# Weight-gradient partials of w2: from a DRAM round trip to sums held open in PSUM, with layer 1's 1−tanh on VectorE

## The chip, the cores and the metric

The kernel runs on one core of one Trainium2 chip. The metric is the device time of one launch in microseconds; lower is better. Engine names as in the profile: PE is the tensor engine (PEld its weight loads), DVE the vector engine, ACT the scalar engine, POOL GpSimd, SP the sync engine. POOL, SP and ACT also issue DMAs, each from its own queue of instructions.

## The reference

The model has two layers, each a gated long convolution (A) and an MLP (B), both with a residual and a LayerNorm ahead of them. S = 2048, D = 448, F = 1792, all inputs bf16. The kernel computes the output and the gradients of all inputs but the constant `B_x`, for a given `grad_out`.

```python
def _A_ref(q, k, v, shift_k, ssm_k, ssm_D):
    k_shift = ...                      # 4-tap causal shift convolution of k
    kv = k_shift * v
    kv_f, kf_f = rfft(kv, 2S), rfft(ssm_k, 2S)
    y = irfft(kv_f * kf_f)[:S] + kv * ssm_D
    return q * y
def _B_ref(x, w1, w2):
    return silu(x @ w1) @ w2
x = A_q
x = x + _A_ref(_layernorm(x), A_k, A_v, A_shift_k, A_ssm_k, A_ssm_D)
x = x + _B_ref(_layernorm(x), B_w1, B_w2)
x = x + _A_ref(_layernorm(x), A_k, A_v, A_shift_k, A_ssm_k, A_ssm_D)
x = x + _B_ref(_layernorm(x), B_w1, B_w2)
out, vjp = jax.vjp(f, ...); return (out, *vjp(grad_out))
```

The gradient of `w2`, a matrix of 1792 x 448, is the sum over both layers of (silu activations, transposed) times (the gradient at the layer's output). In each layer that is a contraction over the 2048 positions. The gradient of `w1` has the same form.

## The kernel before

The convolution's result y is the same in both layers (it does not depend on x), so it is computed once, in a prefix (0 to about 97 us of the trace). `Main` then runs layer 0 forward (about 97 to 212), layer 1 forward with layer 1 backward interleaved (to about 420), and layer 0 backward (to about 554). `_ssm_suffix` takes the gradient gYb, summed over both layers, through the FFT convolution backward and does the rest of the weight gradients.

**Main.** The 2048 positions are four chunks of 512. For one chunk, `h` multiplies by w1 (ps_h, L556), takes tanh (L560) and silu (L561) on ACT, and forms the derivative dT on DVE (L564, L569, L570). Between them stands 1−tanh: in layer 1 it is on ACT (L566), in layer 0 on DVE (L568). `out` multiplies by w2 (ps_o, L588). `ga` (ps_g, L618) multiplies the output gradient by w2T; ACT copies that out of PSUM (L624), DVE multiplies it by dT (L625). `gn` (ps_n, L659) multiplies by w1T and goes through the backward of two LayerNorms on DVE, per 128 positions: ACT reads ps_n into lb_u (L661), and DVE runs `ln_bwd` (L639 to L643) and L668 to L671. w2T and w1T lie in the pool "mwt", which closes when Main ends.

**Weight gradients.** One sum for 128 rows of w2 (index ft, 0 to 13) is ps_d: 16 matmuls of 128x448, one for each 128 positions, with the activations (dstat, 512 KB, loaded by SP from DRAM, for half of layer 0's by a transposing DMA) as the stationary side and the output gradient as the moving side. For layer 1 (activations A_d1) the moving side is grad_out; for layer 0 (activations A0_d) it is mov2, the gradient at layer 0's output, cast at L697.

- `_wgrad_w2_first` makes the mov2 x A0_d part for ft 0 to 9 at the end of Main and for ft 10 to 13 after FFT stage 1 in the suffix. ACT copies each ps_d to dpo in fp32 (L804), and POOL stores it in W2P_d (L805, 224 KB).
- `_wgrad_rest` makes the grad_out x A_d1 part (L795) from the spectrum stage on. It loads the partial again (dpart, L816, on SP), adds it on DVE (L821) and stores the bf16 result. After that come the w1 sums: both layers' parts in one PSUM sum of 32 matmuls, then a cast (L826), transposes (L829), a scaled copy on ACT (L831) and a store.

**Suffix.** FFT stage 1 is `_fft_stage1` (ps_s, L209; it needs M1s, loaded on POOL, and gYb) with its copy to A1g; then transposes (ps_tr, L873); then, for seven pairs of chunks (cp), `spectrum` (L883), the products pa and pb with kk_c (L908, L909; kk_c is loaded on POOL by `kernel_part`, L893 and L894) and the inverse matmuls (ps_v, L229 and L230). Then gK (L949), gkv, sk (L980), gk (L998). POOL also loads ksf (L896, at cp 2) and mov3 (L898, at cp 4). The ps_d matmuls have no fixed places among this: a scheduler orders the instructions, and may put them between others. `issue_after` gives the earliest place.

PSUM places go by tags with two buffers each: "mm" (ps_h, ps_g, ps_s, ps_tr and most of the suffix), "tr" (ps_t, ps_d) and "po" (ps_o, ps_n, ps_sk, ps_dt).

The lines that decide a sum:

```python
def fin_w2(ft, ps, part):
    o = pool.tile([P, D], BF16, name="dout", tag="dout", bufs=4)
    nc.vector.tensor_tensor(out=o[:], in0=ps[:, :D], in1=part[:], op=ALU.add)
    nc.gpsimd.dma_start(out=k.outs[8][ft * P:(ft + 1) * P, :], in_=o[:])
```

Of the kernel before, what the change touches and what calls it, by code (L numbers as in the profile page):

```python
# [10 lines left out]
FP32 = mybir.dt.float32  # L11
# [6 lines left out]
P = 128  # L18
S = 2048
D = 448  # L20
# [100 lines left out]
def kernel(  # L121
# [41 lines left out]
    k.W2P_d = dram.tile([F, D], FP32, name="W2P_d")  # L163
# [20 lines left out]
    with tc.tile_pool(name="yk", bufs=1, side="right") as yk:  # L184
        k.Ysb = yk.tile([P, J, D], BF16, name="Ysb")
        _ssm_prefix(k)
        k.w1sb = k.wk.tile([DC, ND, F], BF16, name="w1sb", tag="WA")
        nc.sync.dma_start(out=k.w1sb[:], in_=k.B_w1.rearrange("(c p) f -> p c f", p=DC))
        k.w2sb = k.wk.tile([P, NF, D], BF16, name="w2sb", tag="WB")
        nc.sync.dma_start(out=k.w2sb[:], in_=k.B_w2.rearrange("(c p) d -> p c d", p=P))  # L190
        k.psum = ctx.enter_context(tc.tile_pool(name="psum", bufs=1, space=PSUM, reuse_waits="tile"))
        k.bal.reset()
        with ExitStack() as es:
            m = Main(k, es)
            m.run()
            with tc.issue_after(k.d0_load.ins):
                _wgrad_w2_first(k, m.td, range(10))
# [48 lines left out]
def _pm(ap2d):  # L246
    return ap2d.rearrange("(p j) d -> p j d", j=J)
# [30 lines left out]
def _ssm_prefix(k):  # L278
# [4 lines left out]
    with ExitStack() as es:  # L283
# [16 lines left out]
        ksb += [k.dp.tile([DC, S], BF16, name="K_sb", tag="dstat", bufs=2)[:] for i in range(2)]  # L300
# [116 lines left out]
        k.x0c0 = k.dp.tile([P, 4, D], BF16, name="x0c0", tag="dstat", bufs=2)  # L417
        nc.gpsimd.dma_start(out=k.x0c0[:], in_=_pm(k.A_q[0])[:, 0:4, :])
        k.na0 = k.dp.tile([P, 4, D], BF16, name="na0", tag="dstat", bufs=2)
# [41 lines left out]
class Main:  # L461

    def __init__(self, k, es):
        self.k, self.nc, self.tc = k, k.nc, k.tc
        nc, tc = k.nc, k.tc
        pool = lambda name, **kw: es.enter_context(tc.tile_pool(name=name, bufs=1, reuse_waits="tile", **kw))
        self.wt = pool("mwt")
        self.w2T = self.wt.tile([P, ND, F], BF16, name="w2T")
        self.w1T = self.wt.tile([P, NF, D], BF16, name="w1T")
        self.td = pool("mtd")  # L470
        self.ch = pool("mch")
        self.xp = pool("mx", side="right")
        self.X = self.xp.tile([P, NT, D], FP32, name="X")
        self.w1sb, self.w2sb, self.Y = k.w1sb, k.w2sb, k.Ysb
# [71 lines left out]
    def h(self, c, L, nT, half, hold):  # L546
# [4 lines left out]
        for ft0, n in ((0, 2), (2, 2), (4, 2), (6, 1)) if half == 0 else ((7, 1), (8, 2), (10, 2), (12, 2)):  # L551
# [13 lines left out]
            if L == 1:  # L565
                nc.scalar.activation(tm, tm, ACT.Copy, scale=-1.0, bias=1.0)  # L566
            else:
                nc.vector.tensor_scalar(out=tm, in0=tm, scalar1=-1.0, scalar2=1.0, op0=ALU.mult, op1=ALU.add)  # L568
# [203 lines left out]
def _wgrad(k, pool, bridge, groups, consume, pre=None, alt=False, fts=range(NF)):  # L772
    nc, psum = k.nc, k.psum
    movs = []
    for (stat, mov_src), tag in groups:
        if tag is None:
            movs.append(mov_src)
            continue
        mov = k.wk.tile([P, NT, D], BF16, name="dmov", tag=tag)
        nc.sync.dma_start(out=mov[:], in_=mov_src)  # L780
        movs.append(mov)
    job = -1
    for ft in fts:
        ps = psum.tile([P, 512], FP32, name="ps_d", tag="tr", bufs=2)
        aux = pre(ft) if pre else None
        for gi, ((stat, _), _) in enumerate(groups):
            job += 1
            if pool is None or (job % 2 == 0 if alt else job < bridge or job % 5 < 2):
                pl, bf, tg = k.dp, 2, "dstat"
            else:  # L790
                pl, bf, tg = (pool, 2, "S") if alt else (pool, 3, "dstat")
            st = pl.tile([P, NT, P], BF16, name="dstat", tag=tg, bufs=bf)
            _load_stat(k, st, stat, ft)
            for t in range(NT):
                nc.tensor.matmul(ps[:, :D], lhsT=st[:, t, :], rhs=movs[gi][:, t, :], start=(gi == 0 and t == 0), stop=(gi == len(groups) - 1 and t == NT - 1))  # L795
        consume(ft, ps, aux)


def _wgrad_w2_first(k, pool, fts):
    nc, dp = k.nc, k.dp  # L800

    def consume(ft, ps, aux):
        o = dp.tile([P, D], FP32, name="dpo", tag="dpart", bufs=3)
        nc.scalar.copy(o[:], ps[:, :D])  # L804
        nc.gpsimd.dma_start(out=k.W2P_d[ft * P:(ft + 1) * P, :], in_=o[:])  # L805

    _wgrad(k, pool, 0 if pool else NF, [((k.A0_d, k.mov2), None)], consume, alt=pool is not None, fts=fts)


def _wgrad_rest(k, pool, after, mov3):  # L810
    nc, dp, psum = k.nc, k.dp, k.psum
    out7v = k.outs[7].rearrange("(c p) f -> p c f", p=DC)

    def pre(ft):
        part = dp.tile([P, D], FP32, name="dpart", tag="dpart", bufs=3)
        nc.sync.dma_start(out=part[:], in_=k.W2P_d[ft * P:(ft + 1) * P, :])  # L816
        return part

    def fin_w2(ft, ps, part):
        o = pool.tile([P, D], BF16, name="dout", tag="dout", bufs=4)  # L820
        nc.vector.tensor_tensor(out=o[:], in0=ps[:, :D], in1=part[:], op=ALU.add)  # L821
        nc.gpsimd.dma_start(out=k.outs[8][ft * P:(ft + 1) * P, :], in_=o[:])

    def fin_w1(ft, ps, aux):
        o = pool.tile([P, D], BF16, name="dout", tag="dout", bufs=4)
        nc.vector.tensor_copy(o[:], ps[:, :D])  # L826
        pt = psum.tile([DC, ND, P], BF16, name="ps_dt", tag="po", bufs=2)
        for dc in range(ND):
            nc.tensor.transpose(pt[:, dc, :], o[:, dc * DC:(dc + 1) * DC], k.ident[:])  # L829
        o7 = pool.tile([DC, ND, P], BF16, name="do7", tag="do7", bufs=2)  # L830
        nc.scalar.activation(o7[:], pt[:], ACT.Copy, scale=0.5)  # L831
        nc.gpsimd.dma_start(out=out7v[:, :, ft * P:(ft + 1) * P], in_=o7[:])

    with k.tc.issue_after(after[-1]):
        _wgrad(k, pool, 4, [((k.A_d1, _pm(k.grad_out[0])), "WA")], fin_w2, pre)
    _wgrad(k, pool, 0, [((k.GH_d[1], mov3), None), ((k.GH_d[0], _pm(k.N_d[1][:])), "WA")], fin_w1)


def _ssm_suffix(k):
# [7 lines left out]
    with ExitStack() as es:  # L847
        pool = lambda name: es.enter_context(tc.tile_pool(name=name, bufs=1, reuse_waits="tile"))
        sp0 = pool("sp0")
        k.M1sb = sp0.tile([P, 16, 2, P], BF16, name="M1s", tag="kk0")  # L850
        with tc.high_priority():
            nc.gpsimd.dma_start(out=k.M1sb[:].rearrange("p a c k -> p (a c k)"), in_=k.m1_h.ap())
# [5 lines left out]
        ksf = sp.tile([P, J, D], BF16, name="ksf")  # L858
# [4 lines left out]
        _wgrad_w2_first(k, None, range(10, NF))  # L863
        mov3 = k.wk.tile([P, NT, D], BF16, name="mov3", tag="WB")
        after = []
        with tc.tile_pool(name="sspec2", bufs=1, reuse_waits="tile") as p1:
# [9 lines left out]
            def spectrum(cp):  # L876
                lo, hi = cp * 2048, (cp + 1) * 2048
                xsw = p1.tile([P, 2048], BF16, name="xsw_c", tag="xsw", bufs=3)
                for u in range(2):
                    ps = psum.tile([P, 1024], FP32, name="ps_s2", **mm)  # L880
                    for hh in range(2):
                        c0 = lo + u * 1024 + hh * 512
                        i = nc.tensor.matmul(ps[:, hh * 512:(hh + 1) * 512], lhsT=k.Gsb[:, G_FWD, :], rhs=Zf[:, c0:c0 + 512], start=True, stop=True)  # L883
                    if cp == 0:
                        after.append(i.ins)
                    _copy(nc, bal.pick(1024), Zf[:, lo + u * 1024:lo + (u + 1) * 1024], ps[:])
                _swap_halves_dma(k, xsw, Zf, lo, hi, nc.scalar, dlo=0)
                return xsw

            def kernel_part(cp):  # L890
                kk = (sp0.tile([P, 2, 2048], BF16, name="kk_c", tag="kk0") if cp % 2 else p1.tile([P, 2, 2048], BF16, name="kk_c", tag="kk1"))
                lo, hi = cp * 2048, (cp + 1) * 2048
                nc.gpsimd.dma_start(out=kk[:, 0, :], in_=k.SPEC_d["K"][:, lo:hi])  # L893
                nc.gpsimd.dma_start(out=kk[:, 1, :], in_=k.SPEC_d["KV"][:, lo:hi])  # L894
                if cp == 2:
                    tc.keep_in_program_order(nc.gpsimd.dma_start(out=ksf[:], in_=_pm(k.KS_d[:])))  # L896
                if cp == 4:
                    tc.keep_in_program_order(nc.gpsimd.dma_start(out=mov3[:], in_=_pm(k.N_d[3][:])))  # L898
                return kk
# [22 lines left out]
        p2 = es.enter_context(tc.tile_pool(name="sp2", bufs=1, reuse_waits="tile"))  # L922
# [17 lines left out]
        gK2 = sp0.tile([DC, 2, S], BF16, name="gK2", tag="kk0")  # L940
# [47 lines left out]
        for g in range(8):  # L988
# [10 lines left out]
            gk = p2.tile([P, 2, D], BF16, name="gk", tag="gk", bufs=3)  # L999
            _copy(nc, bal.pick(2 * D), gk[:], pk[:, :, :D])  # L1000
            nc.gpsimd.dma_start(out=out2_pm[:, 2 * g:2 * g + 2, :], in_=gk[:])
        _wgrad_rest(k, dp2, after, mov3)
# [30 lines left out]
```

## Time and profile before

| | us |
|---|---|
| five runs | 824.29, 825.23, 825.84, 827.11, 831.08 |
| their median | 825.84 |
| the profiled execution | 824.29 |
| its span in the trace | 822.5 |
| last ps_n of Main ends | 537.7 |
| first transpose L873 starts | 582.9 |
| last ps_d of the w1 sums ends | 816.7 |

The span is the time from the first to the last recorded event; 1.8 us of the profiled execution lie around it. The mean granted clock of PE was 0.982 of full speed. In the rows of groups of instructions, the arrow points from the inputs to the output, "x" is the count, then come busy us and mean ns of one, and after the second bar the idle time of that engine just before, with what ended it:

```profile
L795 PE MATMUL ps_d<-dmov,dstat 128*128 128x448 bf16 x448 | 99.0, 356 | 7.8 <-DMA dstat<-A_d 5.5
L659 PE MATMUL ps_n<-w1T,ghT 128*128 128x448 bf16 x448 | 91.3, 352 | 5.7 <-ACT lb_u L661 3.7
L826 DVE CAST dout<-ps_d 128x448 bf16<-128x448 f32 x14 | 8.7, 624 | 83.1 <-PE ps_d L795 83.1
L566 ACT ACTIVATE dT<-dT 128x1024 bf16<-128x1024 bf16 (+1 forms) x32 | 30.6, 964 | 17.9 <-DVE lb_cc L641 17.9
```

Matmuls overlap one another, so the mean of one (356 ns) is longer than the distance between two (189.5 ns where 16 of them take 3.03 us). ACT waited 17.9 us in total ahead of L566, until DVE had got past its LayerNorm backward.

### The profile page before, as it was taken

What the parts mean: (1) busy time and instruction counts of PE and PEld (TensorE: products, weight loads), DVE (VectorE), ACT (ScalarE), POOL (GpSimd) and SP (SyncE); (2) the same over time, 40 slices, a digit from 0 to 9 for tenths busy, and PEclk for the clock granted to TensorE, in tenths of its full rate; (3) what the DMA queues carried; (4) which work ended last, traced back from release to release, by engine and by line L of the source; (5) the groups of instructions that cost most, each with busy time, mean ns of one, the idle gap of its engine ahead of it and who ended that gap; (6) DMA issues with size and microseconds to landing.
All of it is one profiled execution on the core that took longest, in us unless ns stands there. A gap on an engine that the chain in (4) does not pass through costs nothing.

```text
span 822.5 us, 12887 instructions
## 1 busy us (share of the span) xinstructions
PE 751.2 (91%) x4921; PEld 411.0 (50%) x4950; DVE 571.1 (69%) x1252; ACT 455.8 (55%) x577; POOL 153.0 (19%) x225
## 2 busy tenths in 40 slices
PE   6998888999999989969999999999879899999997
PEld 4966543444544444434444444454546575445553
DVE  3789788999874996977968999993456557710000
ACT  4879876787977768577845533324435573201000
POOL 1143223222121011110101010112111141311111
PEclk9999998999999999989999999999989999999999
DMA  9359998685878659649799456499898969797771
GB/s 313 123 182 280 358 228 253 202 263 185 221 181 187 164 158 230 179 112 253 194 276 320 170 155 191 138 266 313 285 304 287 344 239 185 210 282 183 184 176 42
DMA packets 168876, 181.36 MB, mean 220 GB/s; under 512 B 135457, under 2 KB 139169, under 8 KB 167663
## 3 DMA queue, kind: packets, MB, share of 16 engines
q1 hardware_dynamic: 144768, 83.54, 40.1%
q0 software_dynamic: 22304, 92.99, 34.1%
q10 hardware_dynamic: 1742, 4.02, 2.2%
q8 instruction: 38, 0.62, 0.3%
q14 instruction: 24, 0.19, 0.1%
HBM read 69.85 MB, written 70.19 MB: 170 GB/s over the span
## 4 chain that ended last, share of the span: by engine, by line
issue 27%; DVE 24%; PE 18%; ACT 14%; DMA 10%; POOL 6%; POOLq 0%; SPq 0%; DVEq 0%; ACTq 0%
PE ps_d L795 3%; ACT aT L561 3%; DVE lb_u L642 3%; DMA out_dram<-gKD 3%; DVE X L643 3%; DVE lb_junk L639 2%; ACT dT L560 2%; PE ps_h L556 2%; DMA dstat<-A_d 2%; ACT dT L566 2%; PE ps_g L618 2%; DMA kk_c<-spec_KV 2%; DVE dT L570 2%; POOL rstd L264 2%; DVE w1p L569 1%
## 5 line engine op out<-in xcount | busy, mean ns | idle before, releaser
L795 PEld LDWEIGHTS <-dstat 128*128 128x128 bf16 x896 | 86.7, 98 | 88.5 <-DMA dstat<-A_d 7.3
L618 PE MATMUL ps_g<-gT,w2T 128*128 128x512 bf16 x432 | 101.7, 384 | 13.5 <-ACT ghT L624 12.3
L556 PE MATMUL ps_h<-nT,w1sb 112*128 112x512 bf16 x448 | 106.3, 383 | 3.9 <-ACT aT L561 2.3
L795 PE MATMUL ps_d<-dmov,dstat 128*128 128x448 bf16 x448 | 99.0, 356 | 7.8 <-DMA dstat<-A_d 5.5
L659 PE MATMUL ps_n<-w1T,ghT 128*128 128x448 bf16 x448 | 91.3, 352 | 5.7 <-ACT lb_u L661 3.7
L588 PE MATMUL ps_o<-w2sb,aT 128*128 128x448 bf16 x448 | 92.8, 353 | 2.0 <-DVE X L589 1.0
L795 PE MATMUL ps_d<-mov,dstat 128*128 128x448 bf16 x448 | 91.6, 352 | 0.5 <-DMA dstat<-A_d 0.5
L618 PEld LDWEIGHTS <-w2T 128*128 128x128 bf16 x448 | 44.2, 99 | 67.5 <-issue 18.3
L556 PEld LDWEIGHTS <-w1sb 112*128 112x128 bf16 x448 | 43.8, 98 | 57.8 <-issue 12.4
L624 ACT CAST ghT<-ps_g 128x1024 bf16<-128x1024 f32 (+1 forms) x64 | 56.0, 903 | 28.6 <-PE ps_g L618 23.9
L560 ACT ACTIVATE dT<-ps_h 128x1024 bf16<-128x1024 f32 (+1 forms) x64 | 59.1, 923 | 21.2 <-PE ps_h L556 20.5
L659 PEld LDWEIGHTS <-ghT 128*128 128x128 bf16 x448 | 42.7, 98 | 49.3 <-issue 6.1
L826 DVE CAST dout<-ps_d 128x448 bf16<-128x448 f32 x14 | 8.7, 624 | 83.1 <-PE ps_d L795 83.1
L588 PEld LDWEIGHTS <-aT 128*128 128x128 bf16 x448 | 42.6, 98 | 44.3 <-ACT aT L561 4.6
L561 ACT ACTIVATE aT<-ps_h 128x1024 bf16<-128x1024 f32 (+1 forms) x64 | 59.3, 926 | 0.0
L831 ACT ACTIVATE do<-ps_dt 112x512 bf16<-112x512 bf16 x14 | 8.4, 597 | 89.9 <-PE ps_dt L829 89.9
L229 PE MATMUL ps_v<-Gsb,pa 128*128 128x128 bf16 x336 | 44.9, 226 | 6.0 <-DVE pa L908 3.1
L661 ACT ACTIVATE lb_u<-ps_n,rhalf 128x448 f32<-128x448 f32 x32 | 20.5, 640 | 52.5 <-DVE gYb L669 22.0
L230 PE MATMUL ps_v<-Gsb,pb 128*128 128x128 bf16 x336 | 43.5, 226 | 3.1 <-DVE pb L440 2.0
L569 DVE TENSOR_TENSOR w1p<-w1p,aT 128x1024 bf16<-128x1024 bf16 (+1 forms) x64 | 39.6, 618 | 6.9 <-ACT aT L561 6.5
L570 DVE TENSOR_TENSOR dT<-w1p,dT 128x1024 bf16<-128x1024 bf16 (+1 forms) x64 | 39.5, 617 | 3.5 <-ACT dT L566 3.3
L566 ACT ACTIVATE dT<-dT 128x1024 bf16<-128x1024 bf16 (+1 forms) x32 | 30.6, 964 | 17.9 <-DVE lb_cc L641 17.9
(193 smaller groups left out, 1320.4 us busy)
## 6 DMA issues: line engine op xcount, KB each, us to landing
A_d<-turned POOLq DMA_DIRECT2D x12, 896.0 KB, 5.1
dstat<-A_d SPq DMA_DIRECT2D x21, 512.0 KB, 6.2
DT_d<-dT POOLq DMA_DIRECT2D x8, 896.0 KB, 5.1
GH_d<-turned POOLq DMA_DIRECT2D x8, 896.0 KB, 5.9
dTl<-DT_d SPq DMA_DIRECT2D x8, 896.0 KB, 6.1
GH_d<-ghT POOLq DMA_DIRECT2D x8, 896.0 KB, 7.9
dstat<-GH_d SPq DMA_DIRECT2D x14, 512.0 KB, 3.7
spec_K<-Z POOLq DMA_DIRECT2D x7, 512.0 KB, 7.6
```

Of the source, the lines that this page charges most:

```text
L229: nc.tensor.matmul(pv[:, i, :], lhsT=pa[:, i * P:(i + 1) * P], rhs=k.Gsb[:, ga, :], start=True, stop=False)
L556: nc.tensor.matmul(ps[:, u, :], lhsT=self.w1sb[:, dc, ft * P:(ft + 1) * P], rhs=nT[:DC, dc, :], start=(dc == 0), stop=(dc == ND - 1))
L560: nc.scalar.activation(tm, ps[:, 0:n, :], ACT.Tanh, scale=-0.5)
L561: nc.scalar.activation(a, ps[:, 0:n, :], ACT.Silu)
L566: nc.scalar.activation(tm, tm, ACT.Copy, scale=-1.0, bias=1.0)
L569: nc.vector.tensor_tensor(out=wv, in0=wv, in1=a, op=ALU.mult)
L570: nc.vector.tensor_tensor(out=tm, in0=wv, in1=tm, op=ALU.add)
L588: i = nc.tensor.matmul(po[:, :D], lhsT=aT[ft // 7][0][:, ft % 7, tl * P:(tl + 1) * P], rhs=self.w2sb[:, ft, :], start=(ft == 0), stop=(ft ...
L618: nc.tensor.matmul(ps[:, u, :], lhsT=self.w2T[:, b, ft * P:(ft + 1) * P], rhs=gT[:, b, :], start=(b == 0), stop=(b == ND - 1))
L624: nc.scalar.copy(v, ps[:, u[0]:u[0] + len(u), :])
L659: nc.tensor.matmul(pn[:, :D], lhsT=ghT[ft // 7][:, ft % 7, tl * P:(tl + 1) * P], rhs=self.w1T[:, ft, :], start=(ft == 0), stop=(ft == NF - 1))
L795: nc.tensor.matmul(ps[:, :D], lhsT=st[:, t, :], rhs=movs[gi][:, t, :], start=(gi == 0 and t == 0), stop=(gi == len(groups) - 1 and t == NT ...
```

## The change

Both layers' parts of one w2 sum now go into one PSUM sum, as the w1 sums already have it.

- `W2P_d`, the stores to it, the loads from it and the fp32 add are gone. A `Wgrad` class holds the work. `hold` opens four sums (ft 0 to 3) on layer 0's part (A0_d x mov2) at the end of Main, in the places "tr", "tr", "po", "po", and keeps them. `w2` closes them with A_d1's part in the suffix; for ft 4 to 13 it does both parts there in one go, then a cast on DVE and the store.
- The pool of w2T and w1T lives to the end of the kernel. grad_out for the sums (mov1) is loaded on ACT's queue into w2T's place after Main. M1s, then every odd kk_c, then gK2, go into w1T's place, where they had a pool "sp0" of their own.
- ksf goes into gYb's place and is loaded at cp 5. mov3 and both dmov loads go: the two moving sides of the w1 sums (movn) are loaded on POOL after gk, into the place of the gk stage's pool.
- dstat has three buffers in each of its pools; dout has three (it had four), do7 one (two), gk two (three).
- In layer 1, 1−tanh is on DVE, as in layer 0.

The core of the diff (cut):

```diff
-                _wgrad_w2_first(k, m.td, range(10))
+            k.wg = Wgrad(k)
+            k.mov1 = k.wt.tile([P, NT, D], BF16, name="mov1", tag="w2T")
+            nc.scalar.dma_start(out=k.mov1[:], in_=_pm(k.grad_out[0]))
+            k.M1sb = k.wt.tile([P, 16, 2, P], BF16, name="M1s", tag="w1T")
+            nc.gpsimd.dma_start(out=k.M1sb[:].rearrange("p a c k -> p (a c k)"), in_=k.m1_h.ap())
+                k.wg.hold(m.td)
...
-            if L == 1:
-                nc.scalar.activation(tm, tm, ACT.Copy, scale=-1.0, bias=1.0)
-            else:
-                nc.vector.tensor_scalar(out=tm, in0=tm, scalar1=-1.0, scalar2=1.0, op0=ALU.mult, op1=ALU.add)
+            nc.vector.tensor_scalar(out=tm, in0=tm, scalar1=-1.0, scalar2=1.0, op0=ALU.mult, op1=ALU.add)
...
+def _wmm(k, ps, st, mov, first, last):
+    for t in range(NT):
+        i = k.nc.tensor.matmul(ps[:, :D], lhsT=st[:, t, :], rhs=mov[:, t, :], start=first and t == 0, stop=last and t == NT - 1)
+    return i.ins
...
+    def stat(self, pool, tag, bufs, src, ft):
+        k = self.k
+        if pool is None or self.job % (bufs + 3) < 3:
+            st = k.dp.tile([P, NT, P], BF16, name="dstat", tag="dstat", bufs=3)
+        else:
+            st = pool.tile([P, NT, P], BF16, name="dstat", tag=tag, bufs=bufs)
+        self.job += 1
+        _load_stat(k, st, src, ft)
+        return st
+
+    def hold(self, pool):
+        for ft in range(4):
+            st = self.stat(pool, "S", 2, self.k.A0_d, ft)
+            ps = self.k.psum.tile([P, 512], FP32, name="ps_d", tag=("tr", "po")[ft // 2], bufs=2)
+            self.last = _wmm(self.k, ps, st, self.k.mov2, True, False)
+            self.held.append(ps)
+
+    def w2(self, pool, mov):
+        k, nc = self.k, self.k.nc
+        for ft in range(NF):
+            if ft < 4:
+                ps = self.held[ft]
             else:
+                ps = self.k.psum.tile([P, 512], FP32, name="ps_d", tag="tr", bufs=2)
+                _wmm(k, ps, self.stat(pool, "dstat", 3, k.A0_d, ft), k.mov2, True, False)
+            _wmm(k, ps, self.stat(pool, "dstat", 3, k.A_d1, ft), mov, False, True)
+            o = pool.tile([P, D], BF16, name="dout", tag="dout", bufs=3)
+            nc.vector.tensor_copy(o[:], ps[:, :D])
+            nc.gpsimd.dma_start(out=k.outs[8][ft * P:(ft + 1) * P, :], in_=o[:])
...
-            _fft_stage1(k, n2, k.gYb[:, n2, :], A1, psum)
-        _wgrad_w2_first(k, None, range(10, NF))
-        mov3 = k.wk.tile([P, NT, D], BF16, name="mov3", tag="WB")
+            _fft_stage1(k, n2, k.gYb[:, n2, :], A1, psum)
+        ksf = k.wk.tile([P, J, D], BF16, name="ksf", tag="WB")
...
-                if cp == 2:
+                if cp == 5:
                     tc.keep_in_program_order(nc.gpsimd.dma_start(out=ksf[:], in_=_pm(k.KS_d[:])))
-                if cp == 4:
-                    tc.keep_in_program_order(nc.gpsimd.dma_start(out=mov3[:], in_=_pm(k.N_d[3][:])))
...
-        _wgrad_rest(k, dp2, after, mov3)
+        es2.close()
+        with tc.issue_after(k.wg.last):
+            k.wg.w2(dp2, k.mov1)
+        p3 = pool("sp3")
+        mov = [p3.tile([P, NT, D], BF16, name=f"movn{i}") for i in range(2)]
+        for L in (1, 0):
+            nc.gpsimd.dma_start(out=mov[L][:], in_=_pm(k.N_d[2 * L + 1][:]))
+        k.wg.w1(dp2, mov)
```

In the order of instructions, the last two ps_n groups of Main now follow each other directly; behind them come the 16 ps_d of ft 2, four L209 matmuls, 40 ps_d, and then L209 with ps_d between. 123 ps_d stand ahead of the first transpose L873 (224 before), 12 to 17 between each two groups of transposes (none before), and 561 after the last gk (477 before). The counts of PE's instructions are the same.

## The prediction

> **What bounds the kernel now.** I read the page first (busy rows), then the view of waits for the tensor engine, then the two stretches that it points to, in the timeline and in windows of one or ten us. The page's slices:
>
> ```profile
> PE 751.2 (91%) x4921; PEld 411.0 (50%) x4950; DVE 571.1 (69%) x1252; ACT 455.8 (55%) x577; POOL 153.0 (19%) x225
> PE   6998888999999989969999999999879899999997
> PEclk9999998999999999989999999999989999999999
> DMA  9359998685878659649799456499898969797771
> ```
>
> PE bounds it: 751.2 of 822.5 us. Nothing in the change takes a matmul away (the order of instructions shows 4950 before and after, 896 of them ps_d), so what can be won are idle gaps and half-speed stretches: 66.6 us idle between instructions by the timeline, plus 4.7 at the end. Of these 5.1 at the start and some 25 in the forward pass are not touched. What the rest waits for:
>
> ```profile
> PE ps_g L618 <- ACT ghT L624: 12.3, 6, 6.9
> PE ps_d L795 <- DMA dstat<-A_d: 6.0, 3, 4.7
> PE ps_v L229 <- DVE pa L908: 3.1, 1, 3.1
> PE ps_d L795 <- DMA dmov<-N_d: 1.9, 1, 1.9
> ACT dT L566 <- DVE lb_cc L641: 17.9, 3, 8.4
> ```
>
> (us in total, times, longest.) The first and the last belong together. ACT's timeline near 348 us:
>
> ```profile
> 348.21 1.58 ACT L566 ACTIVATE dT<-dT 128x512 bf16<-128x512 bf16 x2 [8.40 <-DVE lb_cc L641]
> ...
> 353.25 1.04 ACT L566 ACTIVATE dT<-dT 128x1024 bf16<-128x1024 bf16 x1
> 354.20 1.89 ACT L624 CAST ghT<-ps_g 128x1024 bf16<-128x1024 f32 x2
> ```
>
> ACT stands 8.40 us before a 1−tanh (L566) that needs DVE to have read tanh (L564); DVE is full with LayerNorm backward just then, and the PSUM copies L624 queue behind. PE waits 6.87 us for them, to 355.2, and runs at half clock to 359.6:
>
> ```profile
> 340.00:350.00 10.00, 8.31 (x41) 4.01 (x41) 9.96 (x28) 1.79 (x3) 1.58 (x2) 1.00 0.66 210
> 350.00:360.00 10.00, 4.77 (x13) 1.72 (x13) 10.00 (x19) 7.71 (x10) 0.55 (x1) 0.66 0.11 46
> 610.00:620.00 10.00, 5.23 (x34) 3.02 (x36) 1.75 (x4) 2.92 (x3) 0.00 (x0) 0.66 0.91 370
> ```
>
> (Columns: window, PE, weight loads, DVE, ACT, POOL, clock, DMA share, GB/s.) DVE's 9.96 and 10.00 tell what sets the pace there; in 610–620 every engine idles and only DMA works (0.91): that is the 4.73 us wait for dstat.
>
> **The change, part by part** (minus is faster).
>
> 1. *1−tanh of layer 1 from ACT to DVE: −6.0.* It takes 32 instructions, 30.6 us, from ACT (24 full ones of 1067 ns, eight halves) and gives DVE 32 as in L568: 24 of 428 ns and 8 of about 276 = 12.5 us busy, about 0.34 us each in pace when back to back. The stall of L624 goes, but what is late next is DVE itself. One chunk (55.4 to 56.9 us apart) is a loop: LN backward on DVE, LN statistics, rstd on POOL, normalising on ACT, transposes, ps_h, tanh and silu on ACT, back to DVE. In the part of that loop that ACT paces (371.8 to 381.0) three L566 of 0.94 us pace go (2.8), and ps_h starts about 0.8 earlier (an estimate: most of one L566 stands in ACT's order ahead of what it needs): −3.6. In the part that DVE paces, 0.2 + 3 × 0.34 = 1.2 are added, and some 0.5 where halves fall in: +1.7. Net −1.9 per chunk, three chunks, and a last −0.3 in the chunk that has no successor: −6. Bounds: −9.5 (near two thirds of the 14.8 us that PE idles in layer 1) and −2 (only the last chunk and part of one). The half-clock stretch lies beside DVE's work and is worth nothing more.
>
> 2. *From the last ps_n (537.7) to the transposes L873 (582.9 now): +6.1, and +1.0 for the clock.* Before the first transpose PE now does 224 ps_d, afterwards 123: 101 go behind it, 101 × 0.1895 us (16 take 3.03) = 19.1 us; they are not saved. If nothing else changed, transposes would start at 563.8. Against that:
>  - Held ft 2 and 3 need the two "po" banks, which ps_n of the last chunk holds until lb_u has read them:
>
> ```profile
> 540.20 0.63 ACT L661 ACTIVATE lb_u<-ps_n,rhalf 128x448 f32<-128x448 f32 x1 [1.59 <-DVE gYb L669]
> ...
> 546.13 0.64 ACT L661 ACTIVATE lb_u<-ps_n,rhalf 128x448 f32<-128x448 f32 x1 [1.42 <-DVE gYb L669]
> ```
>
>  PE has nothing else in its order: 537.7 to 540.9, 3.2 idle.
>  - M1s takes w1T's place, so its load is issued after the last ps_n, not at 531.5. It landed in 8.2 us: about 546. The 16 ps_d of ft 2 end at 544: 2.0 idle before L209.
>  - The closing A_d1 part of ft 0 loads on SP behind A0's ft 6, which waits for a buffer freed about 553; it lands about 560, wanted at 558: 1.8. Behind it on SP stand only further dstat loads.
>  - The first A1g copy on DVE waits for the end of LN backward (554.2): 0.6.
>  - The 1.65 us gap at 563.8 (L209 waits for A1g on ACT) goes, since ps_d now lies between these matmuls: −1.5.
>  Sum 6.1. Bounds 2 (loads land at once) and 12 (M1s in 14.2 us, as ksf at its worst).
>  *The clock.* In the rows a gap of 2.79 us (296.3) left the clock at 1.00, one of 3.10 (651.6) gave 0.50 from 656.3 to 659.6, one of 4.73 gave 0.50 up to 618.8, 4.2 us after work began again. The Trainium skill, "TensorE: Matmul & The Clock Gate", section "Why this matters for your kernels", allows no gaps over about 3 us, at the price of a return to half rate. That speaks against a 3.2 us hole: by the rule a 3.4 us window at half rate, 1.7 lost; by the nearest rows 0 or 1.65. I take 1.0.
>  *The held banks.* The skill's "PSUM — Partial Sum Buffer", section "Summary: rules for kernel authors", says to evacuate promptly, and four sums held from 541 to about 575 is the opposite. It gives no price; by the trace no other tile with tags "tr" or "po" is wanted until the sums close (L209 and L873 use "mm"), so the row's 3.2 us is all I charge.
>
> 3. *Transposes L873: −1.5.* Between them stand now 12 to 17 ps_d each. The gaps at 584.8 to 592.6 (0.42, 0.82, 1.06, 1.10) go, but three dout casts (624 ns, DVE) come between the Zg copies, some 1.6 back, and 1.5 is left. Bounds 0 and −3.4.
>
> 4. *dstat waits: −5.5, and −2.1 of clock.* Partials of 224 KB were written 14 times and read 14 times, 6.4 MB; the DMA row of that stretch shows 0.9 to 1.0 at 4.73's wait. That traffic, the ksf burst (cp 2 to cp 5) and the dmov load leave it, and A0's and A_d1's loads use three and three buffers from the start. 0.80 + 4.73 = 5.5. The half-clock stretch to 618.8 goes with it: half of 4.2. Bounds: 0 (another load is late there) and −7.6; I take the full value, as from 696 to 720 ps_d waits for no dstat at a DMA share of 0.75.
>
> 5. *kk_c: −1.5.* At 651.6 pa waited for kk_c(6), queued on POOL behind mov3 (13.6 us to land). mov3 goes, but ksf (14.2 us) now stands ahead of the same kk_c. Bounds −3.9 (3.10 and the 0.8 after) and 0; nearer the row that repeats, so less than half.
>
> 6. *dmov wait: −1.9.* The two movn tiles (1.8 MB each, POOL, after gk) have 113 ps_d = 21.4 us of w2 sums as cover; such loads landed in 7.9 to 13.6. Without cover: up to 10.
>
> 7. *Hidden:* 14 ACT copies (532 ns), 14 POOL issues (0.54), 14 SP loads; the DVE add (624 ns) becomes a cast of 624 ns. SP's dmov loads go; ACT's queue gains one (mov1, after Main, place free from about 520, wanted at 552). gk with two buffers and do7 with one lie beside ps_d runs; if not, below 1 us each at 14 places is 14, which only the last few can show. The 1.29 at gk, 0.72 and 4.7 at the end stay.
>
> **Sum:** −6.0 + 7.1 − 1.5 − 7.6 − 1.5 − 1.9 = −11.4. The profiled execution took 824.29 us (span 822.5, 1.8 around it), so 812.9 on its scale. It was the fastest of five, 1.55 under their median of 825.84; on the median's scale **814.4**.
>
> **Rivals.**
> - *More (0.15):* layer 1 gives its 9.5, kk_c all 3.9: −3.5 − 2.4 → 808.5. For it: DVE is busy only 164 of 208 us of the stage. Against: it is full just where the loop closes.
> - *No change (0.20):* layer 1 gives only 2 (+4.0), and a load is late again at the place of the old dstat wait (+5.5): 823.9. For it: DMA share 0.9 through 560–660. Against: 6.4 MB less.
> - *Slower (0.12):* DVE becomes layer 1's bound outright. All 12.5 us of L568 land on its chain instead of winning 6: +18.5 → 832.9. Place: 326–362 and its two like; it decides from about 9.6 of the 12.5 (above 830). For it: DVE 9.96 and 10.00 of 10, and the chain there is DVE line after line. Against: most L568 fall outside such stretches.
> - That the change doesn't do what it says: the order shows partials and their loads gone; only the held part could be undone, and isn't.
>
> **How the numbers follow.** Likeliest 0.53, its own range 808.5 to 820.5. About 0.5% (4.1 us) is what a measurement of this kernel tells from no change: 821.7 to 830. Likeliest and "more" lie under it: 0.68; same 0.20; slower 0.12. For 8 in 10 the range runs from 805 (a little under "more") to 828 (past "no change", short of slower).
>
> **What would show it.** Layer 1: no ACT wait on lb_cc at dT, no PE gap over 3 us, its stage 6 us shorter. PE idle of about 3.2 at 531 and 2.0 before the first L209 (times 6 earlier), transposes some 13 earlier relative to the last ps_n. No dstat wait over 1 us in the spectrum stage, a clock of 1.00 there. A short pa wait at kk_c(6); none on movn. Wrong if PE gaps over 3 us stand in layer 1, if the last ps_n isn't earlier, or if dstat or kk_c waits of over 4 us stand behind the transposes.

## The result, and the profile after

The changed kernel takes 833.12 us (median of 43 runs, 827.02 to 844.21), the kernel before 827.38 us in the same sessions (80 runs). The ratio is 1.0061, with a 95% interval of 1.0045 to 1.0076: slower by 5 us, where 11 us less was forecast. (The ratio leaves out of both sets the slow executions, those more than 1.5% above the kernel's fastest, so it is not the quotient of the two medians.) The profiled execution took 838.0 us (span 836.2), so it lies 5 us above its own median. Where it is used below, other profiles show which parts of it repeat.

The page after, engines and slices. A digit is the busy share of one fortieth of the span in tenths (9 is 90% or more), and in the row PEclk the granted clock:

```profile
PE 757.9 (91%) x4921; PEld 412.9 (49%) x4950; DVE 578.5 (69%) x1284; ACT 422.9 (51%) x531; POOL 145.1 (17%) x212
PE   6998788999988999989998699977999799999995
PEclk9999898999998999999999889998999899999998
DMA  9369897685895659769799956638689696897760
```

PE is still 91% busy. ACT lost 33 us and DVE got 7: the edits did what they say. But PE's row now has a 6 in slice 23 and 7s in slices 27 and 28, where it had 9s; the DMA row falls to 3 in slice 27; and the clock shows eight slices below 9 where it showed three. Below, a hole is a stretch in which PE stands idle, and line numbers are those of the kernel that a row comes from. The waits of PE (us in total, times, longest):

```profile
PE ps_n L661 <- DVE ghT L627: 9.8, 9, 4.3
PE ps_g L620 <- ACT ghT L626: 8.6, 6, 4.9
PE ps_d L776 <- DMA dstat<-A_d: 5.7, 1, 5.7
...
PE ps_v L234 <- DVE pa L890: 4.9, 1, 4.9
...
PE ps_d L776 <- ACT lb_u L663: 3.8, 2, 3.1
```

The 6.87 us wait for ghT has become one of 4.9 at another place. The dstat wait has moved, from the spectrum stage to FFT stage 1. The wait for pa is 4.9 where it was 3.1. The last row is the wait for the held sums' place, predicted at 3.2 us. The first row has grown from 2.0. By stages, from the starts and ends of matmuls in both traces:

| stage | before | after | difference | predicted |
|---|---|---|---|---|
| start to first ps_g of layer 1 | 242.3 | 245.6 | +3.3 | 0 |
| layer 1, first ps_g to last ps_n | 186.9 | 186.0 | −0.9 | −6.0 |
| layer 0 backward, to its last ps_n | 108.6 | 116.1 | +7.5 | 0 |
| to the first transpose L873 | 45.1 | 36.6 | −8.5 | −12.0 |
| to the first ps_v | 16.5 | 16.6 | 0.0 | +1.7 |
| to the last ps_v | 66.7 | 62.7 | −4.1 | −9.1 |
| to the last ps_d | 150.5 | 163.0 | +12.5 | +14.0 |
| end, behind the last PE instruction | 4.7 | 8.6 | +3.9 | 0 |

(The predicted column spreads the sum over stages: 101 postponed matmuls are 19.1 us less ahead of the transposes, and later 17 of them come back between transposes and first ps_v, and 84 in the tail. The last ps_d to the last PE instruction is the same.) The first row was not touched by the change and is +0.4 to +0.7 in the profiles of the first four experiments, so most of it is this execution's own.

Five places carry the difference. A row of the timeline has the start, the length, the engine (with q: its queue of instructions), line, operation and count, and in brackets the idle time before it with what ended it. In layer 1's first chunk, GpSimd, DVE and ACT of the changed kernel:

```profile
246.26 0.98 POOL L486 DMA_DIRECT2D A_d<-turned  x1 [6.55 <-DMA turned<-aT]
247.26 1.03 POOL L269 TENSOR_TENSOR rstd<-ln_ve,mhalf 128x4 f32<-128x4 f32 x1
```

```profile
248.32 0.16 DVE L271 SCALAR_TENSOR_TENSOR ln_nmr<-ln_mv,rstd 128x4 f32<-128x4 f32 x1 [4.00 <-POOL rstd L269]
```

```profile
248.52 2.71 ACT L276 ACTIVATE nb<-X,ln_nmr,rstd 128x448 bf16<-128x448 f32 x4 [10.77 <-DVE ln_nmr L271]
251.42 1.68 ACT L595 CAST ob<-X 128x1792 bf16<-128x1792 f32 x1 [0.19 <-DVE X L591]
253.01 1.92 ACT L626 CAST ghT<-ps_g 128x1024 bf16<-128x1024 f32 x2
```

and GpSimd and ACT of the kernel before at the same place:

```profile
241.11 0.98 POOL L481 DMA_DIRECT2D A_d<-turned  x1 [2.63 <-DMA turned<-aT]
242.15 1.03 POOL L264 TENSOR_TENSOR rstd<-ln_ve,mhalf 128x4 f32<-128x4 f32 x1
```

```profile
243.41 1.41 ACT L271 ACTIVATE nb<-X,ln_nmr,rstd 128x448 bf16<-128x448 f32 x2 [5.81 <-DVE ln_nmr L266]
244.73 1.67 ACT L593 CAST ob<-X 128x1792 bf16<-128x1792 f32 x1
246.31 1.91 ACT L624 CAST ghT<-ps_g 128x1024 bf16<-128x1024 f32 x2
```

GpSimd has the small power operation rstd behind a store of A_d, and that store waits 6.55 us for its transposing loads (2.63 before, in the same order). DVE waits for rstd, ACT for DVE, and the first ghT copy starts 7.4 us after the first ps_g (253.01 against 245.58); before it was 4.0. PE stands from 249.2 to 254.1. In the chunk, PE gained a hole of 4.87 us with a half-clock stretch behind it, and in the third chunk the hole of 6.87 shrank to 1.72.

In layer 0's backward pass, SyncE and DVE:

```profile
434.74 32.86 SPq L765 DMA_TRANSPOSE dstat<-A_d  x4
467.70 0.53 SPq L687 DMA_DIRECT2D dTl<-DT_d  x1
```

```profile
476.37 0.43 DVE L627 TENSOR_TENSOR ghT<-dTl,ghT 128x512 bf16<-128x512 bf16 x1 [6.86 <-DMA dTl<-DT_d]
```

The four loads for the held sums took SyncE 32.9 us to issue (one alone 16.2), and the derivative of the second chunk stands behind them. In the kernel before, the same four loads stand ahead of it, but one goes out earlier and together they take 18.1:

```profile
418.28 5.24 SPq L763 DMA_TRANSPOSE dstat<-A_d  x1
...
431.02 12.85 SPq L763 DMA_TRANSPOSE dstat<-A_d  x3
443.97 0.75 SPq L685 DMA_DIRECT2D dTl<-DT_d  x1
```

In FFT stage 1, PE and SyncE:

```profile
573.99 0.93 PE L776 MATMUL ps_d<-mov,dstat 128*128 128x448 bf16 x2 [5.73 <-DMA dstat<-A_d]
```

```profile
555.34 9.51 SPq L765 DMA_TRANSPOSE dstat<-A_d  x2
565.03 3.97 SPq L771 DMA_DIRECT2D dstat<-A_d  x4
```

The closing loads (L771, from A_d1) go out at 565.0, behind two transposing loads (L765, from A0) that wait for buffers. For 24 us SyncE issues nothing but these two. The wait that the prediction's step 2 set at 1.8 us is 5.73.

At the last kk_c, DVE and GpSimd:

```profile
655.50 0.69 DVE L890 TENSOR_TENSOR pa<-Zg,kk_c 128x1024 bf16<-128x1024 bf16 x1 [5.92 <-DMA kk_c<-spec_KV]
```

```profile
635.22 0.53 POOL L880 DMA_DIRECT2D ksf<-KS_d  x1
...
642.82 0.53 POOL L877 DMA_DIRECT2D kk_c<-spec_K  x1 [1.70 <-DVE pb L891]
643.33 0.53 POOL L878 DMA_DIRECT2D kk_c<-spec_KV  x1
```

ksf's 1.8 MB went out 7.6 us ahead of kk_c, whose slower half took 12.0 us to land; the median of such loads from 620 to 665 us is 7.0. In the kernel before, behind mov3, the same half took 12.1.

Last, the end. In the instructions of the closing line, GpSimd's drain (count, then shortest, median and longest ns), after and before:

```profile
L1018 POOLq DRAIN  x3: 46/107/6850, 828.6 to 836.0; - x3
```

```profile
L1028 POOLq DRAIN  x3: 46/103/2960, 818.8 to 822.2; - x3
```

After its last store GpSimd takes 6.85 us to come to rest, where it took 2.96.

### The profile page after: what moved, and what is told of

Read it like the earlier page. It is cut to its first block, busy times and chain, and to the rows that moved or that the text cites. A ratio compares the mean times of both kernels' runs of the same rounds, so it can differ in the third digit from the quotient of the medians.

```text
span 836.2 us, 12757 instructions
## 1 busy us (share of the span) xinstructions
PE 757.9 (91%) x4921; PEld 412.9 (49%) x4950; DVE 578.5 (69%) x1284; ACT 422.9 (51%) x531; POOL 145.1 (17%) x212
## 4 chain that ended last, share of the span: by engine, by line
DVE 37%; PE 23%; issue 16%; DMA 9%; ACT 8%; POOL 4%; POOLq 0%; SPq 0%; ACTq 0%; DVEq 0%
PE ps_d L776 5%; DVE lb_u L644 4%; DVE X L645 4%; DVE lb_junk L641 4%; DVE w1p L571 3%; DVE dT L572 3%; PE ps_g L620 3%; DVE ghT L627 2%; PE ps_h L561 2%; PE ps_n L661 2%; DVE w1p L569 2%; DVE lb_u L673 2%; DVE dT L570 2%; PE ps_gk L981 2%; POOL rstd L269 2%
## 5 line engine op out<-in xcount | busy, mean ns | idle before, releaser
L776 PE MATMUL ps_d<-mov,dstat 128*128 128x448 bf16 x448 | 101.1, 359 | 9.8 <-DMA dstat<-A_d 5.7
L661 PE MATMUL ps_n<-w1T,ghT 128*128 128x448 bf16 x448 | 94.8, 360 | 13.1 <-DVE ghT L627 9.8
L776 PE MATMUL ps_d<-movn,dstat 128*128 128x448 bf16 x448 | 87.0, 352 | 0.0
L561 PEld LDWEIGHTS <-w1sb 112*128 112x128 bf16 x448 | 44.0, 99 | 59.4 <-issue 14.4
L234 PEld LDWEIGHTS <-pa 128*128 128x128 bf16 x336 | 34.5, 103 | 12.7 <-DVE pa L444 6.2
```

Source lines behind the costliest of these rows:

```text
L234: nc.tensor.matmul(pv[:, i, :], lhsT=pa[:, i * P:(i + 1) * P], rhs=k.Gsb[:, ga, :], start=True, stop=False)
L561: nc.tensor.matmul(ps[:, u, :], lhsT=self.w1sb[:, dc, ft * P:(ft + 1) * P], rhs=nT[:DC, dc, :], start=(dc == 0), stop=(dc == ND - 1))
L661: nc.tensor.matmul(pn[:, :D], lhsT=ghT[ft // 7][:, ft % 7, tl * P:(tl + 1) * P], rhs=self.w1T[:, ft, :], start=(ft == 0), stop=(ft == NF - 1))
L776: i = k.nc.tensor.matmul(ps[:, :D], lhsT=st[:, t, :], rhs=mov[:, t, :], start=first and t == 0, stop=last and t == NT - 1)
```

## Experiments

All ratios are against the kernel before, timed on the same chip beside each run. The changed kernel's own is 1.0061.

**1 and 2. The move of 1−tanh alone, and undone.** Run 1 is the kernel before with

```diff
-            if L == 1:
-                nc.scalar.activation(tm, tm, ACT.Copy, scale=-1.0, bias=1.0)
-            else:
-                nc.vector.tensor_scalar(out=tm, in0=tm, scalar1=-1.0, scalar2=1.0, op0=ALU.mult, op1=ALU.add)
+            nc.vector.tensor_scalar(out=tm, in0=tm, scalar1=-1.0, scalar2=1.0, op0=ALU.mult, op1=ALU.add)
```

and run 2 is the changed kernel with the four removed lines in place of the new one.

> The kernel before with one edit: layer 1's 1-tanh on VectorE; partials, pools and loads as before. Theory A (the move to VectorE is good by itself, and the 4.9 us hole in layer 1's first chunk of the changed kernel is an accident of that execution or comes with the rest of the change): about 6 to 7 us faster than before, near 821, no wait of ACT for lb_cc at dT. Theory B (the move puts the rstd of the first backward chunk behind a store of A_d on GpSimd's queue, so the move itself gives back what it wins): within 2 us of before, and a hole of 4 to 5 us after 15 ps_g of the first chunk.

> The changed kernel with 1-tanh of layer 1 back on ACT; everything else as changed. Theory A: about 6 slower than the changed kernel (near 839), waits for lb_cc at dT again (17 us) and a hole near 7 us in ps_g. Theory B: within 2 us of the changed kernel.

Run 1: ratio 1.0001 (0.9975 to 1.0027). Run 2: 1.0075 (1.0040 to 1.0110). The move is worth nothing in either kernel: theory B. Run 1's trace has a hole of 6.39 us in the first chunk and one of 1.71 in the third; run 2's has 1.98 and 7.02. The hole is moved, not removed, and it is not an accident of one execution.

**3 and 4. Two queue orders of the changed kernel.** Run 3 lets the held sums' loads go out later on SyncE:

```diff
-            if c == 0:
+            if c == 1:
                 k.d0_load = i
```

Run 4 puts ksf behind the last kk_c:

```diff
-                if cp == 5:
+                if cp == 6:
                     tc.keep_in_program_order(nc.gpsimd.dma_start(out=ksf[:], in_=_pm(k.KS_d[:])))
```

> The changed kernel, but the four transposing loads of the held sums may be issued on SyncE only after the derivative load of layer 0's second backward chunk, not after that of its first. Theory C (these four loads stand as 33 us on SyncE ahead of that derivative load, VectorE waits 6.9 us for it and PE stands in three holes of 6.5 us with a half-clock stretch after): 6 to 8 us faster than the changed kernel, stage from the last ps_n of layer 1 to the last ps_n of layer 0 about 109 us instead of 116. Rival (the long transposing loads were a congestion of that one execution): under 2 us of difference in the median.

> The changed kernel with the 1.8 MB load of ksf behind the last kk_c on GpSimd's queue instead of ahead of it. Theory D (the last kk_c takes 12 us to land because ksf stands ahead of it; PE waits 4.95 us for pa there): that hole goes, kk_c lands in about 7 us, 4 to 6 us faster than the changed kernel, unless ksf is then late for g_k's shift product, which would show as a wait of VectorE at the first gkv. Rival (the DMA engines are simply full there): the hole shrinks by less than 2 us.

Run 3: 1.0027 (1.0005 to 1.0049), 2.8 us under the changed kernel, less than theory C said and with intervals that overlap. Its stage, layer 0 backward, is 109.1 us without a hole over 1.3 us, but so is that of run 4 (109.1), which still has the changed kernel's order. The 7.5 us are therefore not in every execution.

The traces show more about these loads. With 1−tanh on ACT (the kernel before and run 2) the four take SyncE 18.1 and 17.9 us, and the stage is 108.6 and 109.2. With 1−tanh on DVE and the order as it was, they take 26.1 to 34.8 us (the changed kernel, runs 1 and 4, and below 10 and 11), and the stage is 109.1 to 116.1. Run 1 holds no sums and still has 33 us there and a stage of 111.3. So in these traces the loss comes with the move of 1−tanh, not with the held sums; why the loads then take longer stays open.

Run 4: 0.9974 (0.9946 to 1.0001), 7.2 us under the changed kernel, a little more than theory D said. The pa wait is gone:

```profile
638.20 0.53 POOL L877 DMA_DIRECT2D kk_c<-spec_K  x1 [1.69 <-DVE pb L891]
638.73 0.53 POOL L878 DMA_DIRECT2D kk_c<-spec_KV  x1
639.25 0.53 POOL L880 DMA_DIRECT2D ksf<-KS_d  x1
```

kk_c now leads, DVE's next pa follows without a DMA wait, and the stage from the first to the last ps_v takes 55.4 us instead of 62.7: the 4.95 us hole and its half-clock stretch. ksf was not late for anything. This hole is not new with the change: it is 3.10 us in the kernel before and 4.74 and 4.75 in runs 1 and 11, where mov3 stands ahead of the same kk_c.

**5. Both together.**

> The changed kernel with both repairs: transposing loads of the held sums after the derivative load of layer 0's second backward chunk, and ksf behind the last kk_c. If the two are separate losses they add: 2.8 (e3) + 7.2 (e4) faster than the changed kernel, near 0.994 of before. If ksf behind kk_c was mainly luck of one session, the ratio is near 1.00.

0.9978 (0.9954 to 1.0001): no better than run 4 alone. The order of run 3 adds nothing here.

**6. The closing loads first.** On top of run 5, the loads of later sums keep their place in the program on SyncE, so A0's ft 6 no longer stands ahead of the closing loads:

```diff
         self.job += 1
-        _load_stat(k, st, src, ft)
+        i = _load_stat(k, st, src, ft)
+        if self.job > 8:
+            k.tc.keep_in_program_order(i)
         return st
```

> As the kernel with both repairs, and on SyncE's queue the transposing load of A0's ft 6 stands behind the loads of the closing parts of ft 0 and 1 instead of ahead. Theory E (my step 2: these loads are late because they stand behind a transposing load that waits for a buffer): the wait of PE for dstat in the first FFT stage, 5.5 us, falls to under 1.5 and the kernel is 4 us faster. Rival F (their place in memory, in a pool over LayerNorm's, comes free only with the end of LayerNorm backward on VectorE, or the loads are slow because four of them and Minvs go out at once): the wait shrinks by 1 us or less.

0.9888 (0.9857 to 0.9919), 0.9% under run 5: theory E, and more than it said. SyncE in this run:

```profile
546.96 1.89 SPq L765 DMA_TRANSPOSE dstat<-A_d  x1
550.79 3.79 SPq L771 DMA_DIRECT2D dstat<-A_d  x3
```

The first of the closing loads goes out 3.8 us behind the one transposing load that is left ahead of them, and the second and third at 553.8 and 554.2, while LayerNorm backward runs on until 555.4; so rival F falls. PE's wait for dstat, 6.84 us in run 5, is not there at all, and the stage from the last ps_n to the transposes is 29.0 us instead of 39.0.

**7. The store that rstd waited behind.** On top of run 5:

```diff
-        nc.gpsimd.dma_start(out=dst[:, 7 * hh:7 * hh + 7, 4 * c:4 * c + 4, :], in_=an[:])
+        (nc.sync if dst is self.k.A_d1 and c == 0 and hh == 1 else nc.gpsimd).dma_start(out=dst[:, 7 * hh:7 * hh + 7, 4 * c:4 * c + 4, :], in_=an[:])
```

> As the kernel with both repairs, and the store of A_d1 for the first chunk's second half is issued by SyncE instead of GpSimd. Theory G (VectorE in layer 1's first chunk waits for the rstd on GpSimd, which stands behind this store, which waits for its transposing loads; ACT's ob and the ghT copies then follow late): the hole of 5 to 6 us after 15 ps_g shrinks to 2 to 3 us, 3 us faster. Rival H (ACT's order, which now has four nb and ob ahead of the first ghT copy where it had two nb and ob, decides): rstd is earlier but the hole stays above 4 us.

0.9898 (0.9863 to 0.9933), 0.8% under run 5. GpSimd and ACT:

```profile
239.45 1.03 POOL L269 TENSOR_TENSOR rstd<-ln_ve,mhalf 128x4 f32<-128x4 f32 x1 [3.43 <-DVE ln_ve L267]
```

```profile
246.85 1.92 ACT L626 CAST ghT<-ps_g 128x1024 bf16<-128x1024 f32 x2
```

rstd waits only for its own input. The copy starts 4.1 us after the first ps_g, with the same four nb and ob ahead of it, so it is theory G, and the order on ACT (rival H) does not decide. PE's hole is 1.50 us, and layer 1 takes 179.6 us: 7.3 less than before the change.

**8. The last store.** On top of run 5:

```diff
-            nc.gpsimd.dma_start(out=out7v[:, :, ft * P:(ft + 1) * P], in_=o7[:])
+            (nc.sync if ft == NF - 1 else nc.gpsimd).dma_start(out=out7v[:, :, ft * P:(ft + 1) * P], in_=o7[:])
```

> As the kernel with both repairs, and the very last store of g_w1 goes out on SyncE instead of GpSimd. Theory I (the end grew from 4.7 to 8.6 us because GpSimd's final drain takes 6.9 us where it took 3.0, after its last store): the drain begins 6 us earlier and the end is back near 4.7, 3 to 4 us faster. Rival J (the last store's own landing sets the end): no change at the end.

0.9909 (0.9874 to 0.9943). The end behind PE is 3.94 us instead of 8.60. GpSimd's drain is still 6.77 us long, but starts one store earlier, beside the last sum: theory I. (The gain of 0.7% is more than the 4.7 us, 0.6%, that the end shows; the interval covers both.)

**9 and 10. All five, and all but the first.** The edits are those above.

> The changed kernel with all five repairs: held sums' transposing loads later, ksf behind the last kk_c, A0's ft 6 behind the closing loads on SyncE, the first chunk's A_d1 store on SyncE, the last store on SyncE. If each of the last three is a wait of its own, their gains over the kernel with the first two add (0.9 + 0.8 + 0.7 per cent): near 0.974 of before, some 805 to 808. If they are partly the spread of single sessions, 0.98 to 0.985.

> All repairs but the first: the four transposing loads stand again ahead of the derivative load of layer 0's second chunk on SyncE. If the 6.5 us of holes there in the changed kernel's profile were usual, 3 to 8 us slower than with all repairs; if they were one execution's congestion, under 1.5 us.

Run 9: 806.71 us, ratio 0.9727 (0.9684 to 0.9771). The three gains of runs 6 to 8 add, so they are separate waits. Run 10: 0.9766 (0.9710 to 0.9821); its profile has one hole of 1.24 us behind the derivative in layer 0's backward pass. The order of run 3 may be worth 3 us, but neither pair of intervals parts here. Run 9's page and waits:

```profile
PE 750.2 (93%) x4950; PEld 408.2 (51%) x4950; DVE 577.4 (72%) x1284; ACT 422.7 (52%) x531; POOL 144.5 (18%) x210
PE   6998788999999998989999999979999998999997
PEclk9999898999999999999999999999999999999999
```

```profile
PE ps_g L620 <- ACT ghT L626: 5.6, 6, 1.7
...
PE ps_d L776 <- ACT lb_u L663: 3.5, 2, 3.1
```

The clock row has no digit under 9 behind the first fifth (a stretch of 3.4 us at half clock behind the held sums' hole, 535.7 to 539.1, is too short to show there), the longest ghT wait is 1.7 us, dstat and kk_c have left the list, and the held sums' 3.1 us is the longest PE wait that the change still causes.

**11. The repair of run 7 without the rest of the change.** Run 1 with run 7's edit.

> The kernel before with 1-tanh of layer 1 on VectorE (which alone gave nothing) and the first chunk's A_d1 store on SyncE; no other part of the change. Theory G: the gain that my step 1 counted, 6 us, appears now, near 0.992 of before, with no hole over 3 us in layer 1. Rival: the store on SyncE helps only with the rest of the change, ratio 0.998 to 1.00.

0.9950 (0.9922 to 0.9979), 4 us under before, between the two expectations. Layer 1 takes 180.0 us (−6.9), as theory G has it. But its profile gives 4.5 of this back in layer 0's backward pass (113.1 us, two holes of 1.90 and 1.52), where four transposing loads again precede the derivative on SyncE, one of them 11.8 us long.

**12. More buffers for g_k.** In run 9, ACT waits 6.6 us in the g_k stage for an earlier result's store to land, since gk has two buffers (three before), and PE then waits 2.6 for ACT. On top of run 9:

```diff
-            gk = p2.tile([P, 2, D], BF16, name="gk", tag="gk", bufs=2)
+            gk = p2.tile([P, 2, D], BF16, name="gk", tag=("gk", "gkv")[g % 2], bufs=2)
```

> All five repairs, and the results of g_k alternate between their two buffers and the two of gkv, which is done by then: four in place of two. Theory K (ACT waits 6.6 us for the store of an earlier result to land before it may copy the next, and PE 2.6 us for ACT): that wait goes, the stage from the last ps_v to the last ps_d is 2 to 3 us shorter, ratio near 0.970. Rival L (ACT's wait is hidden by ps_d between, and PE stands for another reason): the hole stays, ratio as with the five repairs, 0.973.

0.9753 (0.9719 to 0.9787), not to be told from run 9. ACT waits for no store any more, but PE's hole is only moved:

```profile
PE ps_gk L983 <- DVE gkp L977: 2.6, 1, 2.6
```

Now DVE's products are waited for at the stage's start, by the same 2.6. The stage from the last ps_v to the last ps_d is 165.8 us instead of 166.4. Neither theory had it so: the buffers did hold PE up, and freeing them bought almost nothing.

## Why the prediction was wrong

The step that failed first is step 1, with its "what is late next is DVE itself"; two terms of step 2 were too small, step 5's gain did not come, and two terms had been put at nothing. All three signs of being wrong that it named came: a hole of 4.87 us in layer 1, the last ps_n at 547.7 instead of 537.7, and a wait of 4.95 for kk_c. The result lies on the slower rival's 832.9 by luck, for its reason is not what the runs show.

**Step 1, layer 1 (−6.0, measured −0.9).** The next thing late was not DVE but rstd on GpSimd, in the first chunk. I had rstd in the loop, as a link, and did not ask what stood ahead of it on its queue. With the store out of rstd's way layer 1 is 6.5 to 7.6 us shorter (runs 7 and 9 to 12). That this is near 6.0 is luck in part: the saving was to come as 1.9 in each of three chunks, but from the kernel before to run 7 the distances between the first ps_g of successive chunks fall by 0.1, 1.0 and 6.4 us. Most of it is the one hole of 6.87, now 1.72, and the half-clock stretch behind it, which the prediction had worth nothing more; the two were not measured apart.

**Step 2, up to the transposes (−12.0, measured −8.5; without the postponed matmuls +7.1, measured +10.6).** The mechanism was right, two terms were mis-sized. The hole for the "po" bank was set at 3.2 and measured 3.12. M1s was set at 2.0 and cost nothing; it landed in time, and a second wait for lb_u of 0.67 stands there instead (2.0 in runs 2, 3, 10 and 12). The closing load behind A0's ft 6 was set at 1.8 and cost 5.73, 5.4 to 9.2 in other runs. I had the queue and the blocker right, but priced the load as landing about 560 at its usual speed, and did not count that both transposing loads come first and that four loads then go out together. The clock was the other term. I set its cost at 1.0 us; from 547 to 584 the mean granted clock was 0.86, and two stretches at half clock lie on work there, 2.7 and 3.4 us long: about 3 lost by estimate.

**Step 3, transposes (−1.5 with the casts).** Right or a little better: 17 more ps_d fit between transposes and first ps_v, 3.2 us of work, and the stretch stayed at 16.6.

**Step 4, dstat in the spectrum stage (−7.6).** Right as to the place: no dstat wait stands behind the first transpose in any run of the changed kernel (runs 1 and 11, without it, have 4.6 and 4.5 us). In the stage's time it shows in full only once kk_c is repaired: 66.7 to 55.4 us in run 4, 11.3 less, where steps 4 and 5 with all their bounds gave at most 11.5.

**Step 5, kk_c (−1.5, measured 1.85 more of hole).** The gain did not come: ksf took mov3's part, 7.6 us ahead of kk_c, and kk_c landed in 12.0 us where it had taken 12.1. Whether the hole grew by the change is not shown, since runs 1 and 11, with mov3 there, have 4.74 and 4.75. My lower bound was 0, and there was no reason to exclude a loss.

**Step 6, dmov (−1.9).** Right: no wait for movn, and the tail is +12.5 for +14.0 in this execution. In runs 2 to 10 and 12 it is +14.4 to +18.0, part of it the waits at gk that step 7 names.

**Step 7, what stays.** "4.7 at the end stay" failed: +3.9. gk's two buffers lie beside other work in the changed kernel (PE does not wait at gk there); in runs 2 to 9 PE waits 1.4 to 3.9 us at that place, and 1.3 before. And the loads of the held sums on SyncE, which the order of instructions showed ahead of the second chunk's derivative, had no step at all; the stage behind them is 7.5 us longer in the profiled execution and 0.5 to 4.5 in the experiments that keep their order with 1−tanh on DVE.

The slower rival named DVE as the bound of layer 1. No run shows that; with the queue repaired, layer 1 gains about what the likeliest case had. What kept the gain away is where DMAs stand on the queues of GpSimd and SyncE: a store ahead of rstd, ksf ahead of kk_c, transposing loads ahead of other loads, and the last store. It is not the sums held in PSUM: their price is the hole of 3.1 us that I charged, and by estimate up to 3 us lost at half clock behind it (1.0 charged).

## What to carry to other kernels

When a trace names an engine as the releaser, look at what stands ahead of that instruction on its own queue: an op of 1 us on GpSimd or a load of 0.3 us on SyncE inherits every wait of the DMA issued before it. After a change, read the new order queue by queue, and for each instruction that waits, ask which short one behind it is on the path. An edit whose idea is sound can measure as nothing, or slower, until these places are cleared: the same change is 0.6% slower, or with five edits that change only where and when DMAs are issued 2.7% faster than before. How much of the 2.7% these edits would give without the change was tried for one of them alone, together with the move of 1−tanh (run 11, 0.5%). The kernel before also has a late kk_c and a last store on GpSimd, so some of the gain may be theirs.

## What the runs showed that was not expected

- GpSimd's final drain is 6.85 us in the changed kernel and 2.96 before, with the same kind of stores ahead of it. In the traces without held sums (the kernel before, runs 1 and 11) one of the last three stores of the w1 sums goes out 2.1 to 2.2 us behind its input, where all the others take 0.29, and the drain is 2.89 to 2.96. In the eleven traces with held sums no such store of GpSimd is late, and the drain is 6.20 to 6.85. A pause of GpSimd that falls before the end in one kernel and into the drain in the other would fit all fourteen; it was not tried, and its cause stays open.
- A transposing load of 512 KB held SyncE for 1.6 to 16.2 us in the same place of the program. In all five traces with 1−tanh on DVE and the four loads together, one of them takes 10.2 us or more; with 1−tanh on ACT none takes over 5.3, and with run 3's edit none over 9.7. The cause stays open.
- A hole can cost more than its length, and not the same each time. From 645 to 665 the mean clock was 0.83 in the changed kernel, and run 4 won 7.2 us for a hole of 4.95. But behind the same hole of 3.12 us at the held sums the clock stays full in runs 2, 3, 10 and 12, is halved for 3.4 us in the changed kernel's profile and in runs 4, 6, 8 and 9, and for 6.8 us in runs 5 and 7.
